# Attention and a routed expert layer on one core: q, k and v in natural token order, six batches of q and k turned by DMA, and a written order of issue

## The chip, the cores and the metric

The kernel runs on one core of one Trainium2 chip. A core has four compute engines that each run their own stream of instructions in order: TensorE (PE in the profile, with its weight loads as PEld), VectorE (DVE), ScalarE (ACT) and GpSimd (POOL). SyncE (SP) issues most of the DMAs here, in order too, and sixteen DMA engines move the data. The metric is the device time of one execution in microseconds, as a median of several runs.

## The reference, cut to what matters

```python
# q, k, v: (8 batches, 8 heads, 576 tokens, 64), f: (8, 8, 576), all float32
scores = q @ k.T / 8                                # per batch and head
cum = np.cumsum(np.log(np.clip(f, 1e-4, 1.0)), -1)
scores = where(causal, -1e9, scores + cum[:, None] - cum[None, :])
attn = softmax(scores)                              # over keys
x[b] = concat over heads of attn @ v                # (576, 512) per batch
logits = x @ w_gate                                 # 8 experts
for each token, in order:                           # sticky routing
    e = argmax(logits) if first token or sigmoid(x @ w_local) < 0.5 else e of the token before
    out = softmax(logits)[e] * (relu(x @ w1[e]) @ w2[e])   # 512 -> 1024 -> 512
```

All products are made of float16 parts: each operand is split into a high part and a low part (the rest), and the products of the parts that count are added up in PSUM.

## The kernel before, in words

**Stages.** Attention runs over eight batches, one after the other, and the batches overlap at their edges. Then the experts run, first two with fixed places, then the other six in the order of their loads. While attention runs, the routing of finished batches is worked out in between.

**Attention of a batch.** Per batch there are 21 units: 20 of 512 score columns and a small one (`d2unit`). A unit goes through stages on different engines: `sc` (TensorE makes scores into a PSUM bank, from the tiles `A` and `B` of q and k, `scores`, line 931), `mx` (VectorE takes the negative maximum, `negmax`, 948), `ex` (ScalarE takes exp, `expo`, 967), `tr` (TensorE transposes P, 984), `hi` (ScalarE casts to float16, 989), `lo` (VectorE makes the rest, 993; in three to five units a batch TensorE subtracts, `sub`, 996, and ScalarE casts, `lo2`, 1001), `av` (TensorE multiplies with v, 963), and for the last unit of a pair `n1` and `n2` (VectorE divides by the sum, 1024 and 1028). PSUM has four banks for scores, two for `tr`, two for the output of `av`.

**Order of tokens.** The 512 main tokens of a batch are loaded two neighbours to a partition (`load_main`, 190: runs of 512 bytes; v in `load_v`, 205: runs of 256 bytes), so keys and queries of one chunk are interleaved. The code undoes that in the access patterns of `queries` and `keys` (919, 924), with `ORD3` and `ORD4` (18), and in a store of P with a step of two (`expo`). The routing works on the tokens in that order and turns them back with small products (`rows`, 1462, `back`, 1508).

**Preparing q and k.** For the batch after the running one, GpSimd splits q and k into parts (`hi_lo`, 352, lines 357 and 361) in a tile `t16`. For batches 1 to 7, TensorE transposes the 36 blocks of each into score banks (`tq`, 505) and ScalarE or VectorE evicts them into `A` (`eq`, 514, 516, 518; the factor of q is applied here); after that a DMA copies the high half of `A` into `B` (`copy_hi`, 419 to 425, `copy_last`, 429). Batch 0 is turned partly by `turn` (406), a DMA transpose of SBUF into SBUF. The output of a batch, x, goes the same way: split by GpSimd, turned by DMA transposes (`xt`, 814; `xlt`, 851), stored to DRAM (820).

**What sets the order.** While the program is built, `issue` (1301) keeps a model of the engines' clocks with estimated costs and picks, step by step, the stage that could start first, with weights and ranks of its own for each batch (`TUNE`, 79). GpSimd's work is doled out by `pump` (364), loads by `ship` (346) and transfers by `hold_back`. What follows attention (the end of the routing, the first expert tiles, weights) is ordered in the same way by `flow` (2148). On the chip, each engine then runs its stream as issued and waits on semaphores.

Of the kernel before, what the change touches and what calls it, by code (L numbers as in the profile page):

```python
# [17 lines left out]
ORD3, ORD4 = (0, 2, 1), (0, 2, 1, 3)  # L18
# [18 lines left out]
SUBS = (7, 11, 14, 16)  # L37


def moves_of(d):  # L40
# [3 lines left out]

# [4 lines left out]
GM, GW = 8, 500  # L49

SW = (-700, 0, 0)
LI = (14, 18)
PX = 6
XI = 3

TS = {"q": (13, 17, 18, 19, 20), "k": (19, 20, 20, 21, 21)}
TE = {"q": "ADDDA", "k": "DAAAD"}

UO = tuple(range(25))
# [36 lines left out]
}  # L96

# [5 lines left out]
def kernel(  # L103
# [13 lines left out]
    B, H, S, D = q.shape  # L117
# [64 lines left out]
    mask(mB, 0.0, 2, [[-1, 2], [-2, 64]], 1, ALU.not_equal, BIG)  # L182
    mask(mA, 0.0, 2, [[1, 2], [2, 64]], -1, ALU.is_ge, -BIG)


# [4 lines left out]
    def load_main(b, nm, C, h0, h1, eng=nc.sync):  # L190
        src = (q, k)["qk".index(nm)]
        eng.dma_start(
            out=LT[b, nm][:, 4 * h0:4 * h1, :].rearrange("p (h C r) d -> p C h (r d)", C=2, r=2)[:, C],
            in_=src[b, h0:h1, C * 256:(C + 1) * 256].rearrange("h (p r) d -> p h (r d)", r=2))

    def load_last(b, nm, eng=nc.sync):
        src = (q, k)["qk".index(nm)]
        for r in range(2):
            eng.dma_start(out=LT[b, nm][r * 64:(r + 1) * 64, 32:36, :],
                              in_=src[b].rearrange("(j r) s d -> r s j d", r=2)[r, 512:576])  # L200
# [4 lines left out]
    def load_v(b, eng=nc.sync, groups=((0, H),), last=True, cs=range(4)):  # L205

        if (b, "v") not in LT:
            new_load(b, "v")
        t = LT[b, "v"]
        for h0, h1 in groups:  # L210
            for c in cs:
                eng.dma_start(out=t[:, 8 * c + h0:8 * c + h1, :],
                              in_=v[b, h0:h1, c * 128:(c + 1) * 128].rearrange("h s d -> s h d"))
        for u in range(2 if last else 0):
            eng.dma_start(out=t[u * 64:(u + 1) * 64, 32:36, :],
                          in_=v[b].rearrange("(m u) s d -> u s m d", u=2)[u, 512:576])
# [14 lines left out]
    for h0, h1 in ((0, 2), (2, 4)):  # L231
        for nm in "qk":
            for C in range(2):
                load_main(0, nm, C, h0, h1)


    for c in range(2):
        nc.gpsimd.memset(QB[0][64:70, 16 * c + 8:16 * c + 16], -1.0)
# [85 lines left out]
    def nop():  # L324
        pass


    queue = deque()
    quota = [0.0]

    bulk = deque()

    held = []

    def hold_back(ready, fn):
        held.append((ready, len(held), fn))

    def let_go(t):
        while held:
            x = min(held)  # L340
            if x[0] > t:
                return
            held.remove(x)
            x[2]()

    def ship(i):
        while bulk and bulk[0][0] <= i and bulk[0][1]():
            bulk.popleft()[2]()
            if i < 99:
                break  # L350

    def hi_lo(hi, lo, t, n):

        m, w = t.shape[1], 1
        for d in t.shape[2:]:
            w *= d
        out = [(m * w, lambda: nc.gpsimd.tensor_scalar(hi, t, 1.0, 1.0, ALU.mult, ALU.mult))]
        for i in range(0, m, n):
            e = min(i + n, m)
            out.append((2 * (e - i) * w,  # L360
                        lambda i=i, e=e: nc.gpsimd.tensor_tensor(lo[:, i:e], t[:, i:e], hi[:, i:e], ALU.subtract)))
        return out

    def pump(left):

        quota[0] += sum(c for c, _ in queue) / max(left, 1)
        while queue and (queue[0][0] <= quota[0] or left <= 0):
            c, fn = queue.popleft()
            quota[0] -= c
            clock["POOL"] = max(clock["POOL"], clock["PE"]) + 1.1 * c  # L370
            fn()
# [11 lines left out]
    def aug_main(b, nm, h0, eng=nc.sync):  # L383
        B, src = Tq[b][nm + "B"], augm[:, b * H + h0:(b + 1) * H]
        if nm == "k":
            eng.dma_start(out=flat(B[64:67, 4 * h0:32]), in_=src.rearrange("j h x -> j (h x)"))
        for c in range(2 if nm == "q" else 0):
            eng.dma_start(out=flat(B[67:70, 16 * c + 2 * h0:16 * c + 16]).rearrange("p (g x) -> p g x", x=64),
                          in_=src.rearrange("j h (a c x) -> j c (h a) x", a=4, c=2)[:, c])
# [16 lines left out]
    def turn(b, nm, h0, h1):  # L406
        t16, A = Tq[b][nm + "t"], Tq[b][nm + "A"]
        if nm == "k":
            nc.sync.dma_start_transpose(out=A[:, 4 * h0:4 * h1], in_=flat(t16[:, 4 * h0:4 * h1]))
            return  # L410
        for c in range(2):
            nc.sync.dma_start_transpose(
                out=A[:, 16 * c + 2 * h0:16 * c + 2 * h1, :].rearrange("p a (r x) -> p (a r) x", r=2),
                in_=flat(t16[64 * c:64 * c + 64, 4 * h0:4 * h1]))
# [4 lines left out]
    def copy_hi(b, nm, h0, h1):  # L419
        A, B = Tq[b][nm + "A"], Tq[b][nm + "B"]  # L420
        if nm == "k":
            nc.sync.dma_start(out=B[0:64, 4 * h0:4 * h1], in_=A[64:128, 4 * h0:4 * h1])
            return
        dst, src = (t[0:64, 0:32].rearrange("p (c h C) x -> p c h (C x)", c=2, C=2)[:, :, h0:h1] for t in (B, A))
        nc.sync.dma_start(out=dst, in_=src)
# [9 lines left out]
    def prep_qk(b, nm):  # L435

        def begin():
            new_prep(b, nm)
            prep_aug(b, nm)
            if nm == "q":  # L440
                scale_q(b, 0, 16)
                clock["ACT"] += 950

        def turns(h0):
            if nm == "q" and h0 == 0:
                scale_q(b, 16, 36)
                clock["ACT"] += 1150
            if nm == "k" and h0:
                turn(b, nm, h0, h0 + 5)
            else:  # L450
                turn(b, nm, h0, h0 + 4)
                if h0:
                    turn_last(b, nm)

        def half(g0, g1):
            R = {}

            def parts(i):
# [212 lines left out]
    def moves(x):  # L671
# [1957 lines left out]
```

## Time and profile before

| | us |
|---|---|
| median of 3 runs | 798.42 |
| lowest and highest | 796.38, 800.25 |
| the profiled execution | 794.33 |
| its span, first to last instruction | 792.6 |

The page of the profile gives each engine's busy time and share of the span, the share in 40 slices, the DMA queues, the chain that ended last and the costliest groups of instructions. A busy time is the union of the instructions' own spans. For TensorE a span goes from a matmul's start to its modelled end, and matmuls overlap, so a busy TensorE isn't one at its peak. "DMA share" is the mean busy share of the sixteen DMA engines; packets of one engine overlap, so it can go above 1. The chain that ended last holds only the last 22 us (stores of the last outputs), so the readings below go by stretches.

### The profile page before, as it was taken

The numbers are of one execution on the slowest core, as the hardware profiler recorded it, in microseconds if no ns is written. First come the engines' busy times: TensorE is split into PE (matmuls) and PEld (weight loads), VectorE is DVE, ScalarE is ACT, GpSimd is POOL, SyncE is SP. The second block draws the span as 40 slices with busy tenths as digits, with TensorE's granted clock in tenths as the row PEclk, the third lists the DMA queues.
The fourth block names the chain that finished last, engine by engine and source line by source line (L and its number), as shares of the span: only waits on it lengthen the run. The fifth ranks groups of instructions, "written<-read, shape, count | busy, mean of one in ns | idle before, by whom it ended". The sixth has DMA issues, their size and how long they took to land. (4 is left out here: it accounts for less than half of the span.)

```text
span 792.6 us, 22037 instructions
## 1 busy us (share of the span) xinstructions
PE 744.1 (94%) x8972; PEld 540.2 (68%) x8972; DVE 496.6 (63%) x1097; ACT 435.6 (55%) x813; POOL 409.5 (52%) x525
## 2 busy tenths in 40 slices
PE   5799979998998989988899999999999999999996
PEld 2687868787887868877684576675665757666453
DVE  6789869899988989799769734252450514325010
ACT  5798969797886968875634125242341524324121
POOL 9799989395986779759608414222302213030101
PEclk9999999999999999998999999999999999999998
DMA  7968998877959677295594395574482854727101
GB/s 180 190 144 196 202 188 183 169 142 168 168 139 165 154 154 135 49 197 154 108 223 184 84 266 138 162 213 160 137 206 78 200 168 163 204 89 201 42 2 51
DMA packets 195338, 122.01 MB, mean 154 GB/s; under 512 B 135099, under 2 KB 171197, under 8 KB 195212
## 3 DMA queue, kind: packets, MB, share of 16 engines
q1 hardware_dynamic: 189169, 101.42, 57.0%
q0 software_dynamic: 6064, 19.14, 7.1%
q8 instruction: 72, 1.18, 0.6%
q14 instruction: 33, 0.27, 0.1%
HBM read 72.15 MB, written 19.36 MB: 115 GB/s over the span
## 5 line engine op out<-in xcount | busy, mean ns | idle before, releaser
L969 ACT ACTIVATE P<-st,nm 128x512 f32<-128x512 f32 (+3 forms) x288 | 153.3, 587 | 25.4 <-DVE nm L949 20.2
L1766 PE MATMUL z<-xT,wh 128*128 128x300 f16 (+7 forms) x832 | 144.6, 289 | 0.3 <-DVE hl L1753 0.3
L949 DVE TENSOR_REDUCE nm<-st 128x1 f32<-128x512 f32 (+4 forms) x264 | 133.8, 543 | 12.7 <-PE st L945 5.5
L989 ACT CAST ph<-pt 128x512 f16<-128x512 f32 (+1 forms) x200 | 115.8, 584 | 39.4 <-PE pt L984 33.8
L984 PE MATMUL pt<-ident,P 128*128 128x128 f32 x784 | 123.9, 281 | 9.1 <-DVE pl L993 5.7
L993 DVE TENSOR_TENSOR pl<-pt,ph 128x512 f16<-128x512 f32 (+1 forms) x171 | 114.0, 671 | 15.1 <-ACT ph L989 11.5
L1758 POOL DMA_INDIRECT out_dram<-o,ranki x23 | 23.9, 1039 | 160.9 <-ACT o L1757 139.8
L1753 DVE SCALAR_TENSOR_TENSOR hl<-z,hh 128x240 f16<-128x240 f32 (+7 forms) x64 | 42.3, 662 | 96.3 <-ACT hh L1752 94.7
L984 PEld LDWEIGHTS pt<-ident,P 128*128 128x128 f32 x784 | 85.3, 143 | 24.6 <-DVE pl L993 6.6
L1793 PE MATMUL y<-uh,hh 128*128 128x512 f16 (+2 forms) x440 | 101.1, 310 | 0.3 <-ACT o L1757 0.2
L1793 PE MATMUL y<-ul,hh 128*128 128x512 f16 (+2 forms) x440 | 100.8, 309 | 0.0
L1793 PE MATMUL y<-uh,hl 128*128 128x512 f16 (+2 forms) x440 | 100.8, 309 | 0.0
L1766 PEld LDWEIGHTS <-wh 128*128 128x128 f16 x832 | 80.9, 97 | 26.6 <-issue 0.9
L1766 PE MATMUL z<-xT,wl 128*128 128x300 f16 (+7 forms) x416 | 94.4, 289 | 0.0
L1793 PEld LDWEIGHTS <-hh 128*128 128x128 f16 (+2 forms) x880 | 57.0, 100 | 53.4 <-issue 5.4
L963 PE MATMUL xp<-VH,pl 128*128 128x65 f16 (+1 forms) x960 | 90.5, 195 | 2.5 <-DVE pl L993 1.8
L963 PE MATMUL xp<-VH,ph 128*128 128x65 f16 (+1 forms) x960 | 91.7, 196 | 0.0
L963 PE MATMUL xp<-VL,ph 128*128 128x65 f16 (+1 forms) x960 | 91.2, 195 | 0.0
L963 PEld LDWEIGHTS <-ph 128*128 128x128 f16 (+1 forms) x1920 | 84.6, 102 | 7.6 <-issue 4.0
L1752 ACT ACTIVATE hh<-z 128x240 f16<-128x240 f32 (+7 forms) x64 | 36.7, 574 | 91.7 <-PE z L1766 87.4
L938 PE MATMUL st<-KB,QB 70*128 70x256 f16 (+4 forms) x448 | 77.2, 280 | 4.3 <-DMA KB<-Ak 4.3
L938 PE MATMUL st<-Ak,Aq 128*128 128x256 f16 (+4 forms) x448 | 77.0, 282 | 2.9 <-ACT P L969 2.5
(371 smaller groups left out, 1407.4 us busy)
## 6 DMA issues: line engine op xcount, KB each, us to landing
stg<-in_moe_w_dram SPq DMA_DIRECT2D x64, 512.0 KB
xs<-xr SPq DMA_DIRECT2D x16, 512.0 KB
ldq<-in_q_dram SPq DMA_DIRECT2D x14, 512.0 KB
ldk<-in_k_dram SPq DMA_DIRECT2D x14, 512.0 KB
ldv<-in_v_dram SPq DMA_DIRECT2D x28, 256.0 KB
QB<-Aq SPq DMA_DIRECT2D x15, 256.0 KB
KB<-Ak SPq DMA_DIRECT2D x15, 256.0 KB
ldv<-in_v_dram SPq DMA_DIRECT2D x20, 64.0 KB
```

The source lines that it names most:

```text
L938: nc.tensor.matmul(st[p0:p0 + m, co:co + n], lhsT=queries(lq, kk, h, c), rhs=rhs, start=(ps == 0 and first and co == col), stop=(ps == 1), ...
L949: nc.vector.tensor_reduce(dst, src, axis=AX.X, op=ALU.max, negate=True)
L963: nc.tensor.matmul(xo, lhsT=a[:, c0:c0 + m], rhs=w[:, vi, :], start=False, stop=(i == n - 1 and jj == 2), skip_group_check=True)
L969: nc.scalar.activation(P[:, c0:c1].rearrange("p (k x r) -> p k r x", r=2, x=64), st[:, c0:c1].rearrange("p (k r x) -> p k r x", r=2, x=64) ...
L984: nc.tensor.matmul(U["pt"][:, i * 128:(i + 1) * 128], lhsT=P[:, i * 128:(i + 1) * 128], rhs=ident, is_transpose=True, start=(i == 0), stop ...
L989: nc.scalar.copy(U["ph"][:, :cols], U["pt"][:, :cols])
L993: nc.vector.tensor_tensor(U["pl"][:, :cols], U["pt"][:, :cols], U["ph"][:, :cols], ALU.subtract)
L1752: nc.scalar.activation(hv, z[:, 0:nh, 0:wd], AF.Relu)
L1753: nc.vector.scalar_tensor_tensor(lv, z[:, 0:nh, 0:wd], 0.0, hv, ALU.max, ALU.subtract)
L1758: nc.gpsimd.indirect_dma_start(out=outf, out_offset=bass.IndirectOffsetOnAxis(ap=scat(t), axis=0), in_=o, in_offset=None, bounds_check=NT ...
L1766: nc.tensor.matmul(z[:, a, 0:wd], lhsT=w[:, d, fc * 128:(fc + 1) * 128], rhs=xT[:, x, a * wd:(a + 1) * wd], start=(i == 0), stop=(i == len ...
L1793: nc.tensor.matmul(y[m * r:m * r + m, 0:w], lhsT=a[:, fc, c0:c0 + m], rhs=u[:, fc, w * r:w * r + w], start=(i == 0), stop=(i == len(prods) ...
```

## The change

- **Layout.** The host hands q, k and v over as (batch, 128 partitions, 36 groups, 64), tokens in natural order (`laid`), so a load reads one contiguous run per partition. `queries`, `keys`, `ORD3`, `ORD4`, `expo`, the masks, the copies of q, the decay rows and the routing's products follow; a batch's v is loaded by three DMAs and q and k by three each.
- **Turning.** For batches 2 to 7, `prep_turned` issues two DMA transposes each for q and k (`turn`, 16 and 20 blocks) in place of `tq` and `eq`; ScalarE scales q before the split (`scale_q`, two instructions a batch). Batch 1 is still turned by TensorE (`by_tensor`).
- **Order.** The scheduler, its costs and weights are gone. `ORDER` has one letter for each step of attention, `THEN` one for each step of what follows; `issue` and the last loop read them off. Each step still waits on semaphores on the chip.
- **Routing.** `rows` has two products in place of four, `back` and the carries one each on full 128-row tiles, and the reordering copy `so` is gone.

```diff
-ORD3, ORD4 = (0, 2, 1), (0, 2, 1, 3)
+ORD3, ORD4 = (0, 1, 2), (0, 1, 2, 3)
...
+PARTS = dict(zip("SMNETHLUKARW tc 0123hz gr d. qkfuy xjils vbpe".replace(" ", ""), (
+    "sc mx mn ex tr hi lo sub lo2 av n1 n2 tq eq z0 z1 z2 z3 zh zl gate side due next "
+    "Tq Tk qs cq ck X L x l s v b p e").split()))
+ORDER = (
+    "SSMSMddMEddSTEMSHSdLTEMAHdSLTEMAHSMETLESHMSELTAEMSHMTSEMALHdSRELTWSHMTEALHSUREWTKMSHMdTEMAAHLtTEtLAcMHAcLRTSTW"
...
+THEN = (
+    "gggbbgbhhhbbbggbbbbbihbbgbbbcjgghjbbgbhhhhhgghbgbhhbhbbibbgdhjhbjjjbhhhiibhbbhbigbggbbggkkbbbbgghgjbbbbgebggbb"
...
     def load_main(b, nm, C, h0, h1, eng=nc.sync):
         src = (q, k)["qk".index(nm)]
-        eng.dma_start(
-            out=LT[b, nm][:, 4 * h0:4 * h1, :].rearrange("p (h C r) d -> p C h (r d)", C=2, r=2)[:, C],
-            in_=src[b, h0:h1, C * 256:(C + 1) * 256].rearrange("h (p r) d -> p h (r d)", r=2))
+        g0, g1 = (4 * (h0 + (h1 - h0) * x // 2) for x in (C, C + 1))
+        eng.dma_start(out=LT[b, nm][:, g0:g1], in_=src[b, :, g0:g1])
...
+    def load_v3(b, c):
+        if c == 0:
+            new_load(b, "v")
+        g0, g1 = ((0, 16), (16, 32), (32, 36))[c]
+        nc.sync.dma_start(out=LT[b, "v"][:, g0:g1], in_=v[b, :, g0:g1])
...
     def turn(b, nm, h0, h1):
         t16, A = Tq[b][nm + "t"], Tq[b][nm + "A"]
-        if nm == "k":
-            nc.sync.dma_start_transpose(out=A[:, 4 * h0:4 * h1], in_=flat(t16[:, 4 * h0:4 * h1]))
-            return
...
+        nc.sync.dma_start_transpose(out=A[:, 4 * h0:4 * h1], in_=flat(t16[:, 4 * h0:4 * h1]))
...
+    def prep_turned(b, nm):
+
+        def begin():
+            new_prep(b, nm)
+            prep_aug(b, nm)
+
+        if nm == "q":
+            part["qs"].extend(lambda g=g: scale_q(b, *g) for g in ((0, 16), (16, 36)))
+        part["T" + nm].extend(lambda h=h: turn(b, nm, *h) for h in ((0, 4), (4, 9)))
+        part["c" + nm].extend([lambda: copy_hi(b, nm, 0, 4), lambda: copy_hi(b, nm, 4, 8), lambda: copy_last(b, nm)])
+        return [begin] + halves(b, nm, 0, 16) + halves(b, nm, 16, 36)
...
-            return t[:kk, 16 * (c % 2) + 2 * h + c // 2]
+            return t[:kk, 4 * h + c]
...
         def expo(P, st, c0, c1, bias):
 
-            nc.scalar.activation(P[:, c0:c1].rearrange("p (k x r) -> p k r x", r=2, x=64),
-                                 st[:, c0:c1].rearrange("p (k r x) -> p k r x", r=2, x=64), AF.Exp, bias=bias)
+            nc.scalar.activation(P[:, c0:c1], st[:, c0:c1], AF.Exp, bias=bias)
...
+    def issue(last=False):
+
+        for x in order:
+            st = PARTS[x]
+            if st in runs:
+                go_on(st)
+            elif st != "next":
+                part[st].popleft()()
+            if st in ("sc", "next") and not last:
+                return
...
         def back():
             R["ps"] = bank()
-            for j, x in enumerate((R["so"].rearrange("p r x -> p (r x)"), R["sc"])):
-                nc.tensor.matmul(R["ps"][:, 0:GC], lhsT=x, rhs=idc[:, j], start=(j == 0), stop=(j == 1),
-                                 skip_group_check=True)
+            nc.tensor.matmul(R["ps"][:, 0:GC], lhsT=scw[:, 0:128], rhs=ident16[:, 0:GC], start=True, stop=True,
+                             skip_group_check=True)
...
+def laid(name, a):
...
+    if name not in ("q", "k", "v"):
+        return a
...
+    main = a[:, :, :512].reshape(b, h, 4, 128, d).transpose((0, 3, 2, 1, 4) if name == "v" else (0, 3, 1, 2, 4))
+    last = a[:, :, 512:].reshape(b, h // 2, 2, 64, d).transpose(0, 2, 3, 1, 4)
+    return _np.concatenate([main.reshape(b, 128, 32, d), last.reshape(b, 128, 4, d)], axis=2)
```

The counts that the prediction uses from the diff: the letters of `ORDER` hold 12 `Tq` and 12 `Tk` (two each for six batches), 12 `qs`, 10 `tq` and 10 `eq` (batch 1 only), and as many attention stages as before (192 `sc`, 200 `tr`, 171 `lo`, 29 `sub`).

## Rows read from the trace of the kernel before

**Rows 1.** The page's first part: busy time, share of the span, instructions.
```profile
PE 744.1 (94%) x8972; PEld 540.2 (68%) x8972; DVE 496.6 (63%) x1097; ACT 435.6 (55%) x813; POOL 409.5 (52%) x525
```

**Rows 2.** By stretch, busy us: PE, PEld, DVE, ACT, POOL; granted clock, DMA share, GB/s.
```profile
28.00:396.30 368.30, 341.08 (x5773) 286.07 (x5774) 321.39 (x768) 291.55 (x596) 284.56 (x344) 0.98 0.77 159
75.50:305.00 229.50, 215.38 (x3701) 182.28 (x3700) 203.01 (x485) 186.77 (x383) 176.29 (x228) 0.99 0.83 167
396.30:793.00 396.70, 386.73 (x3063) 243.72 (x3060) 154.72 (x296) 126.49 (x186) 99.11 (x132) 0.99 0.53 148
160.30:209.50 49.20, 46.52 (x773) 38.77 (x772) 47.51 (x114) 41.39 (x86) 36.55 (x47) 1.00 0.76 157
209.50:245.80 36.30, 35.36 (x686) 30.80 (x684) 32.95 (x81) 29.71 (x61) 28.92 (x33) 1.00 0.72 153
```

**Rows 3.** Waits of PE, DVE and ACT, 20 to 410 us: total, times, longest.
```profile
PE pt L984 <- DVE pl L993: 5.7, 12, 1.1
PE st L938 <- DMA KB<-Ak: 4.3, 2, 3.0
DVE pl L993 <- ACT ph L989: 11.5, 21, 1.5
ACT ph L989 <- PE pt L984: 33.8, 52, 3.2
```

**Rows 4.** Turning q and k, groups by line: count, busy us, mean ns, idle before.
```profile
L505 PE MATMUL st<-ident,t16q 128*128 128x128 f16 x252 | 19.4, 219 | 0.2
L514 ACT ACTIVATE Ak<-st 128x1024 f16<-128x1024 f16 x21 | 21.4, 1034 | 1.1 <-PE st L505 1.1
L514 ACT ACTIVATE Aq<-st 128x1024 f16<-128x1024 f16 (+1 forms) x14 | 11.6, 826 | 0.9 <-PE st L505 0.9
L516 DVE TENSOR_SCALAR Aq<-st 128x1024 f16<-128x1024 f16 x21 | 14.1, 682 | 0.8 <-PE st L505 0.8
L518 DVE COPY Ak<-st 128x1024 f16<-128x1024 f16 (+1 forms) x14 | 7.6, 546 | 0.0
```

**Rows 5.** Timeline of PE, 16 transposes in a row: start, length.
```profile
234.94 1.06 PE L505 MATMUL st<-ident,t16q 128*128 128x128 f16 x16
```

**Rows 6.** ScalarE from SBUF float32, 1024 columns, among the groups by line.
```profile
L1965 ACT ACTIVATE wh<-stg 128x1024 f16<-128x1024 f32 x26 | 27.1, 1048 | 0.4 <-DMA stg<-in_moe_w_dram 0.4
```

**Rows 7.** The transposes of x: SP's issue (ns min/median/max), and a stretch with two.
```profile
L814 SPq DMA_TRANSPOSE xt<-xr x16: 1752/2852/3666, 80.9 to 397.1; - x16
339.59 6.02 SPq L814 DMA_TRANSPOSE xt<-xr  x2
339.60:346.00 6.40, 6.29 (x116) 4.75 (x117) 5.80 (x19) 3.44 (x9) 2.56 (x4) 1.00 1.07 158
```

**Rows 8.** Stretches with a load of q, of k, and of weights.
```profile
259.90:267.00 7.10, 6.84 (x101) 5.72 (x99) 6.91 (x18) 6.50 (x15) 6.93 (x7) 1.00 0.68 175
267.40:275.40 8.00, 7.70 (x149) 6.99 (x147) 6.26 (x21) 6.92 (x16) 3.61 (x5) 1.00 0.59 150
362.00:368.00 6.00, 4.72 (x79) 3.77 (x80) 5.68 (x13) 4.23 (x12) 5.71 (x6) 0.69 0.94 307
```

**Rows 9.** By stretch: TensorE idles, its clock falls; first and last of three.
```profile
248.00:252.00 4.00, 2.19 (x17) 1.27 (x15) 4.00 (x10) 2.93 (x8) 2.83 (x3) 0.96 1.38 220
252.00:256.00 4.00, 4.00 (x30) 3.60 (x31) 3.44 (x8) 2.02 (x4) 3.17 (x4) 0.61 1.36 142
364.00:370.00 6.00, 5.43 (x71) 4.40 (x68) 4.21 (x10) 4.70 (x11) 5.67 (x6) 0.53 0.70 242
```

**Rows 10.** Batch 0's start: a stretch in which TensorE waits for a copy.
```profile
32.00:35.50 3.50, 0.90 (x12) 0.86 (x13) 0.86 (x2) 0.36 (x1) 0.16 (x1) 1.00 1.12 223
```

**Rows 11.** Groups by line and shape: the routing's copy, exp, a contiguous store.
```profile
L1506 DVE COPY so<-sc 10x128 f16<-10x128 f16 x4 | 2.1, 534 | 0.0
L969 ACT ACTIVATE P<-st,nm 128x512 f32<-128x512 f32 x96 | 71.0, 745 | 18.4 <-DVE nm L949 13.7 <-DVE G L1458 1.5 <-ACT ph L989 0.8
L1757 ACT ACTIVATE o<-y,rank 128x512 f32<-128x512 f32 x23 | 15.7, 685 | 81.0 <-PE y L1793 72.1 <-PEq L2576 4.8 <-issue 4.0
```

More of the change, by code (lines that the diff above doesn't have):

```diff
@@ L211, in load_v @@
             for c in cs:
[L212 to L216, printed above, removed]
+                eng.dma_start(out=t[:, 8 * c + h0:8 * c + h1], in_=v[b, :, 8 * c + h0:8 * c + h1])
+        if last:
+            eng.dma_start(out=t[:, 32:36], in_=v[b, :, 32:36])
+    def load_v3(b, c):
[3 more added lines that the diff above has]
+        nc.sync.dma_start(out=LT[b, "v"][:, g0:g1], in_=v[b, :, g0:g1])
     pers = (per0, per1)
@@ L528, in ready @@
-        def ready(js):
-            return (0, lambda: turns.extend(group(j) for j in js))
-        return [(0, begin)] + half(0, 16) + [ready((0, 1))] + half(16, 36) + [ready((2, 3, 4))]
+            part["tq"].append(tq)
+            part["eq"].append(eq)
+        for j in js:
+            group(j)
+            if j in (1, 3):
+                part["c" + nm].append(lambda j=j: copy_hi(b, nm, 2 * j - 2, 2 * j + 2))
+            elif j == 4:
+                part["c" + nm].append(lambda: copy_last(b, nm))
@@ L561, in prep, with loads @@
-        return q + [mark("q")] + k + [mark("k")] + v + last
+        part["p"].extend(prep_turned(b, "q") + prep_turned(b, "k") + prep_v(b))
+        part["v"].extend(lambda c=c: load_v3(b, c) for c in range(3))
+        if b == 2:
+            part["p"].append(init_route)
+        if b + 1 < B:
+            loads(b + 1, "q")
+            loads(b + 1, "k")
+    def loads(b, nm):
+        part["b"].extend([lambda: (new_load(b, nm), load_main(b, nm, 0, 0, H)), lambda: load_main(b, nm, 1, 0, H),
+                          lambda: load_last(b, nm)])
@@ L695, in moves @@
         elif a == "2":
-            c = lambda: all((1, x, j) in turned for x in 'qk' for j in range(4))
-            def some(C):
-                if C == 0:
-                    new_load(2, b)
-                if C < 2:
-                    load_main(2, b, C, 0, H)
-                else:
-                    load_last(2, b)
-            bulk.extend([(0, c, lambda C=C: some(C)) for C in range(3)])
+            loads(2, b)
         elif a == "R":
@@ L1159, in then @@
         def then(i, f, *args):
-            eng, cost, last, takes, frees = units[i]["n2"]
+            last = units[i]["n2"]
             def both():
@@ L1164, in both @@
                 f(*args)
-            units[i]["n2"] = eng, cost, both, takes, frees
+            units[i]["n2"] = both
         for j in range(4):
@@ L1253 @@
-    SHUTS = "add", "rows2", "hold", "scan1", "onehot", "place2", "invert2", "pinvert2", "fill2"
-    chain = deque()
-    side = {"end": (0.0, "PE"), "run": None, "cost": None}
+            then(18, some)
+            then(19, lambda: F[2]())
+        return units
+    pools = {}
+    runs = {"gate": None, "side": None}
     def whole(fn):
@@ L1331, with go_on @@
[L1331 to L1356 removed]
+    def go_on(st):
+        if runs[st] is None:
+            runs[st] = iter(part[st][0]() or ())
+        if next(runs[st], whole) is whole:
+            part[st].popleft()
+            runs[st] = None
@@ L1359 @@
+    order = iter(ORDER)
+    def issue(last=False):
[6 more added lines that the diff above has]
+            if st in ("sc", "next") and not last:
+                return
+    def step(u):
+        for st, fn in u.items():
+            part[st].append(fn)
+        issue()
     GC = NCH // 4
@@ L1719, in early_weights @@
             if n == 0:
-                out += [(0, lambda i=i: load(i)) for i in blocks[0:2]]
+                out += [lambda i=i: load(i) for i in blocks[0:2]]
             if n + 2 < len(blocks):
-                out.append((0, lambda i=blocks[n + 2]: load(i)))
+                out.append(lambda i=blocks[n + 2]: load(i))
             out += pieces(i)
@@ L1801, in experts, with run @@
             f()
-    def run(steps, todo=(), at=None, share=1200):
+    def run(steps, todo=(), at=None):
         todo = list(todo)
@@ L1926 @@
+            if b > 0 and i == 0:
+                part["gate"].extend(gate(b - 1))
                 if b % 2 == 0:
                     steps, EX["rest"] = route(b // 2 - 1, False)
-                    chain.extend(steps)
+                    part["side"].extend(steps)
                 if b == B - 4:
-                    chain.append(first_idx)
+                    part["side"].append(first_idx)
                 if b == B - 2:
-                    chain.extend([early_idx, early_tok])
-    issue()
@@ L1934 @@
-    let_go(1e12)
-    pump(0)
-    ship(99)
-    while chain:
-        side_issue(*side_next())
+                    part["side"].extend([early_idx, early_tok])
+    issue(True)
     pctx.close()
@@ L2242, in fn @@
                 e = n > 1
-                if e and part == 0 and n == 2:
+                if e and which == 0 and n == 2:
                     HID["hh", 1] = ep.tile([128, NF, M1], F16, name="hh")
@@ L2354, in routing, with t2 @@
[L2354 to L2367 removed]
+        def t2():
+            nc.vector.tensor_copy(flat(xlt), R["ps"])
@@ L2394 @@
-    pump(0)
+    streams = dict(zip("bcdefghijklmnop", (
+        products(), hidden(0), hidden(1), outputs(0), outputs(1), routing(), third_pair(), blocks(FW), second(), second_rest(),
+        fetch(CAP4[0] - 4 * EARLY, lambda i: EX["ga"][:, EARLY + i:EARLY + i + 1], "x0"),
+        fetch(CAP4[1] - 4 * EARLY, lambda i: EX["ga"][:, e0 + i:e0 + i + 1], "x1l"), ranking(), third(), steps_of([constants]))))
+    for x in THEN:
+        next(streams[x])
     sidx, xp_, wpb = EX["sa"], EX["xp"], EX["wpb"]
```

831 lines of the change are left out of this document (193 added, 638 removed), and 16 rows, old and new, of the table TUNE.

## The prediction

> **What bounds the kernel now.** I read the page's engine totals first [rows 1]. TensorE looks busy for 94% of the span, but its spans overlap: sixteen transposes in a row take 1.06 us, though each is listed with 219 ns [rows 4, 5]. So one costs (1.06 - 0.22) / 15 = 56 ns of the engine, and the rest is a tail that the busy time counts at every stall. The totals also average over stages, so I went to the stretches [rows 2]. Behind 396.3 us, in the experts, TensorE is busy for 386.7 of 396.7 us and VectorE for 39%: that part is TensorE's own, and the change doesn't touch its products. The change lives in 28 to 396.3 us: eight batches of 46.0 us each. There TensorE is busy for 92.6% (tails included), VectorE for 87.3%, ScalarE 79%, GpSimd 77%. In the batch at 160 us VectorE reaches 96.6%, in the next 90.8%. The waits say that no engine is alone: TensorE waits for VectorE's `pl`, VectorE for ScalarE's `ph`, ScalarE for TensorE's `pt`, each in many short waits [rows 3]. So attention is a ring of TensorE, VectorE and ScalarE, in which VectorE has the most real work, and its length is VectorE's work divided by the share that the order of issue lets it reach. The DMA engines are the fifth party: mean share 0.83 in 75.5 to 305 us [rows 2], and the two waits of scores for a copy into `KB` are theirs [rows 3].
>
> **The change part by part.** First, what leaves. The 504 transposes and 70 evictions belong to seven batches, and six go [rows 4] (k's 252 transposes are a like group). TensorE: 432 x 56 ns = 24.2 us. VectorE: (14.1 + 7.6) x 6/7 = 18.6 us. ScalarE: (21.4 + 11.6) x 6/7 = 28.3 us. Four score banks no longer serve for turning, which can only help.
>
> The routing's copy `so` leaves VectorE 2.1 us, three quarters of it in attention: 1.6 us [rows 11]. The other routing products are a few short ones each; I count nothing.
>
> What comes instead. ScalarE scales q: 1024 and 1280 columns, by the nearest row [rows 6] 1.05 + 1.31 = 2.36 us a batch, 14.1 us for six, so ScalarE is still relieved by 14.2 us; its 21% of idle time covers it. This adds a wait: the scaling waits for q's load, behind it on ScalarE stand the `ex` and `hi` of the running units, and VectorE waits for those; GpSimd's split of q now waits for the scaling, with the splits of k, v and x behind it. Price: nothing if the load is some 10 us old, up to 3.0 us apiece, like the longest wait for a copy [rows 3], if it is late. In the letters the loads stand several units ahead of the scaling, so I take nothing and leave the rest to the range.
>
> The store of exp becomes contiguous. A contiguous ScalarE store of 512 columns takes 685 ns, the strided exp 745 [rows 11]: between nothing and 60 ns a unit, on an engine with idle time, so nothing. Natural order lets some pairs of score products become one with the same columns; the trace doesn't show that a product costs more than its columns, and I count nothing there too.
>
> DMA. A batch's transposes are 2 x 36 blocks. The nearest stretch turns 32 blocks of x in 6.4 us at a share of 1.07 [rows 7], 6.8 us of all sixteen engines, 0.21 us a block, so 15.4 us a batch; SP's shortest issue of 16 blocks, 1.75 us [rows 7], bounds it from below at 7.9. I take the stretch, as it is the same form. The loads shrink: a load of q or k (1.18 MB) takes 0.68 x 7.1 = 4.8 or 0.59 x 8.0 = 4.7 us of the engines [rows 8]; at the rate of the weights, whose rows are contiguous too (307 GB/s at 0.94), it is 3.6 us, so three loads give back 3.5 us (v is read in shorter runs and may give more). DMA time a batch: 0.83 x 45.9 = 38.1 [rows 2], plus 15.4, minus 3.5, is 50.0 us. That fits into 42 us only at a share of 1.19. Rows show 1.12 and 1.38 where much is queued [rows 9, 10]. SP issues four more transposes a batch, 2.85 us each by the median, in order with loads, copies into `B` and the transposes of x, and each of these stands behind a transpose that waits for GpSimd's split. I price the crowding at 1.5 us, between nothing and the 7.8 or more of the rivals below.
>
> [...]
>
> The written order. [...] From below, a share of 85%; from above, the 96.6% of one batch [rows 2]. I take 88%, close to the present mean of 87.3%, as the work on TensorE falls with VectorE's and a batch edge loses its late turning.
>
> The start. Scores wait 3.0 us for the copy into `KB` while the DMA share is 1.12 [rows 3, 10]; shorter loads in batch 0 take away between nothing and 3.0 us: 1.5 us.
>
> What follows attention: TensorE idles for 10 us there [rows 2], the last stores among it; I take nothing.
>
> **The sum.** VectorE's work in attention: 321.4 - 18.6 - 1.6 = 301.2 us. At 88% that is 342.3 us against 368.3: -26.0. Start -1.5, crowding +1.5. Total -26.0, from 794.3 to 768.3 us. From the other side, if TensorE sets the length, its 24.2 us give nearly the same. The profiled execution is 4.1 us below the median of 798.4, so the forecast for a median is 772 us. At 85% attention is 354.4 us (-14, median 784), at 90.8% 331.7 us (-37, 762).
>
> **The rivals.** (1) The order of issue lifts VectorE to 91 to 96.6%: 331.7 to 311.8 us, 742 to 762. For it: batches that reached that [rows 2]. Against it: the DMA time above. (2) The DMA engines become the bound at the share of 1.12 seen at the start [rows 10]: 50.0 / 1.12 = 44.6 us a batch in place of 45.9, so 6 x 1.3 = 7.8 us and the start's 1.5 are all that is won: 789. For it: the sum of DMA time; against it: the 1.38 and 1.36 of [rows 9], and that part of a share is packets that overlap. (3) It doesn't do what it says: the new steps are bound elsewhere or the gain is eaten at the batch edges, 795 to 802. (4) Slower: the DMA engines give no more than a share of 1.0 when transposes, copies and loads alternate. Then a batch takes 50.0 us, 6 x 4.1 - 1.5 = 23 us more: 821. It decides at 50.0 / 45.9 = 1.09: below that share the change loses. [...] For it: 0.83 already, transposes slower than loads by the byte [rows 7, 8]; against it: the shares over 1.1.
>
> [...]
>
> **How the numbers follow.** Forecast (share 85 to 91%) 0.48, rival 1 0.17, rival 2 0.20, rival 3 0.06, rival 4 0.09. Within 0.5% (4 us, about what a measurement of this kernel can tell from no change) is rival 3: 0.06; slower is rival 4: 0.09; faster is the rest, 0.85. The range of 8 in 10 runs from 752 (leaving the upper part of rival 1, some 0.07) to 792 (leaving rivals 3 and 4 for the most part).
>
> **What would show it.** In the profile after: no group for `st<-ident,t16` but batch 1's 72, VectorE's work in attention near 301 us, its share 85 to 91%; attention's last unit some 26 us earlier and the experts' stretch as long as before; DMA share in the middle batches near 1.1 with few waits of scores for `KB` or `QB`. Long waits there, or of ScalarE for `ldq`, mean rival 2 or 4; a share over 91% means rival 1. The prediction is wrong if the experts' stretch changes by more than some us, or if GpSimd, with 77%, turns out to be what the units wait for.

## The result, and the profile after

The changed kernel takes 770.11 us, the median of 4 runs (768.36 to 774.67), beside 797.4 us for the kernel before on the same chip (4 runs, 794.69 to 800.25): a ratio of 0.9666, 95% interval 0.9609 to 0.9723. The forecast was 772. The profiled execution took 768.85 us, its span 766.8.

The page's first part of the changed kernel, the counterpart of [rows 1]:

```profile
PE 716.1 (93%) x8400; PEld 507.9 (66%) x8400; DVE 478.0 (62%) x1055; ACT 416.1 (54%) x795; POOL 409.9 (53%) x515
```

By stretch, with the columns of [rows 2]; attention's last unit now ends at 369.15 us (before at 396.3), and the second line is five whole batches, as 75.5 to 305 us were:

```profile
28.00:369.15 341.15, 316.75 (x5281) 257.56 (x5281) 305.97 (x738) 274.48 (x584) 280.11 (x331) 0.98 0.96 213
70.65:277.53 206.88, 192.98 (x3234) 155.99 (x3232) 186.66 (x456) 171.04 (x366) 169.15 (x207) 0.98 1.01 217
369.15:767.00 397.85, 382.50 (x2987) 239.85 (x2986) 151.80 (x287) 124.24 (x180) 103.95 (x135) 0.98 0.53 147
```

Attention took 341.2 us in place of 368.3, and the experts' stretch 397.9 in place of 396.7. So the whole gain lies in attention. VectorE's work there fell from 321.4 to 306.0 us, TensorE's busy time from 341.1 to 316.8, and the DMA share rose from 0.77 to 0.96.

The groups of turning that are left, the scaling of q and the exp of 512 columns (count, busy us, mean ns, idle before):

```profile
L400 PE MATMUL st<-ident,t16q 128*128 128x128 f16 x36 | 2.7, 219 | 0.1
L378 ACT ACTIVATE ldq<-ldq 128x1024 f32<-128x1024 f32 (+1 forms) x12 | 14.1, 1171 | 1.2 <-DMA ldq<-in_q_dram 1.2
L816 ACT ACTIVATE P<-st,nm 128x512 f32<-128x512 f32 x95 | 65.9, 703 | 9.6 <-DVE nm L890 7.5 <-DVE nm L796 1.5 <-DVE rs L861 0.5
```

The 252 transposes of q are 36, the scaling costs the 14.1 us that were counted and waits 1.2 us in all, and exp takes 703 ns in place of 745.

The waits of 20 to 400 us, as [rows 3], show more waits for copies than before, but short ones:

```profile
PE pt L830 <- DVE pl L839: 3.2, 6, 1.4
PE st L785 <- DMA KB<-Ak: 6.9, 4, 2.1
PE st L785 <- DMA QB<-Aq: 2.7, 2, 1.7
DVE pl L839 <- ACT ph L835: 11.1, 23, 1.5
ACT ph L835 <- PE pt L830: 34.9, 61, 3.5
```

All of this fits the forecast: a share of VectorE of 306.0 / 341.2 = 89.7% where 88% was taken. It doesn't show that VectorE's work is why. The experiments were made for that.

### The profile page after: what moved, and what is told of

Its sections match the earlier page's. It is cut to its first block, busy times and chain, and to the rows that moved or that the text cites. A ratio compares the mean times of both kernels' runs of the same rounds, so it can differ in the third digit from the quotient of the medians.

```text
span 766.8 us, 20737 instructions
## 1 busy us (share of the span) xinstructions
PE 716.1 (93%) x8400; PEld 507.9 (66%) x8400; DVE 478.0 (62%) x1055; ACT 416.1 (54%) x795; POOL 409.9 (53%) x515
## 5 line engine op out<-in xcount | busy, mean ns | idle before, releaser
L816 ACT ACTIVATE P<-st,nm 128x512 f32<-128x512 f32 (+3 forms) x288 | 144.0, 561 | 14.5 <-DVE nm L890 7.5
L835 ACT CAST ph<-pt 128x512 f16<-128x512 f32 (+1 forms) x200 | 113.1, 587 | 36.9 <-PE pt L830 34.9
L830 PE MATMUL pt<-ident,P 128*128 128x128 f32 x784 | 117.7, 281 | 8.2 <-DVE pl L839 3.2
L839 DVE TENSOR_TENSOR pl<-pt,ph 128x512 f16<-128x512 f32 (+1 forms) x171 | 111.9, 667 | 11.9 <-ACT ph L835 11.1
L1434 POOL DMA_INDIRECT out_dram<-o,ranki x23 | 24.2, 1050 | 158.4 <-ACT o L1433 142.1
L1429 DVE SCALAR_TENSOR_TENSOR hl<-z,hh 128x240 f16<-128x240 f32 (+7 forms) x64 | 42.4, 662 | 96.2 <-ACT hh L1428 94.6
L810 PE MATMUL xp<-VH,pl 128*128 128x65 f16 (+1 forms) x960 | 88.8, 195 | 2.6 <-DVE pl L839 2.3
L810 PE MATMUL xp<-VH,ph 128*128 128x65 f16 (+1 forms) x960 | 89.7, 196 | 0.0
L810 PE MATMUL xp<-VL,ph 128*128 128x65 f16 (+1 forms) x960 | 89.3, 195 | 0.3 <-issue 0.3
L810 PEld LDWEIGHTS <-ph 128*128 128x128 f16 (+1 forms) x1920 | 82.6, 103 | 7.5 <-issue 4.0
L785 PE MATMUL st<-KB,QB 70*128 70x512 f16 (+5 forms) x384 | 77.2, 300 | 9.6 <-DMA KB<-Ak 6.9
L785 PE MATMUL st<-Ak,Aq 128*128 128x512 f16 (+5 forms) x384 | 77.1, 303 | 0.8 <-DVE nm L890 0.3
```

Source lines behind the costliest of these rows:

```text
L785: nc.tensor.matmul(st[p0:p0 + m, co:co + n], lhsT=queries(lq, kk, h, c), rhs=rhs, start=(ps == 0 and first and co == col), stop=(ps == 1), ...
L810: nc.tensor.matmul(xo, lhsT=a[:, c0:c0 + m], rhs=w[:, vi, :], start=False, stop=(i == n - 1 and jj == 2), skip_group_check=True)
L816: nc.scalar.activation(P[:, c0:c1], st[:, c0:c1], AF.Exp, bias=bias)
L830: nc.tensor.matmul(U["pt"][:, i * 128:(i + 1) * 128], lhsT=P[:, i * 128:(i + 1) * 128], rhs=ident, is_transpose=True, start=(i == 0), stop ...
L835: nc.scalar.copy(U["ph"][:, :cols], U["pt"][:, :cols])
L839: nc.vector.tensor_tensor(U["pl"][:, :cols], U["pt"][:, :cols], U["ph"][:, :cols], ALU.subtract)
```

## The experiments

Each ratio is to the kernel before, run on the same chip. "DMA time" is DMA share times length, from 28 us to the end of attention's last unit: 283.6 us in the kernel before, 0.96 x 341.2 = 327.5 in the changed one. As the share goes above 1 (1.38 in [rows 9]), it is a measure to compare runs by, not pure work.

### TensorE turns again, with three ways to evict

In the changed kernel, `prep_turned` puts the groups of `by_tensor` behind the same letters, and a small function inserts the letters of `tq` and `eq` into `ORDER` by rule (and leaves out those of `qs`):

```diff
-        if nm == "q":
-            part["qs"].extend(lambda g=g: scale_q(b, *g) for g in ((0, 16), (16, 36)))
-        part["T" + nm].extend(lambda h=h: turn(b, nm, *h) for h in ((0, 4), (4, 9)))
+        part["T" + nm].extend(lambda js=js: by_tensor(b, nm, js) for js in ((0, 1), (2, 3, 4)))
...
+ORDER = spread(ORDER)
```

> The changed kernel (natural layout, contiguous loads, written order), but q and k of batches 2 to 7 are turned by TensorE again, one group of blocks behind an exp, with the evictions shared between VectorE and ScalarE as in the kernel before; the scaling of q goes back into the eviction. Theory W (VectorE's work over its share sets attention's length): VectorE gets 18.6 us back, over a share of 0.90 that is +20.7, less some us for 15.4 us of DMA time a batch that goes: 785 to 791. Theory P (TensorE's work sets it): 432 x 56 ns = 24.2 us over TensorE's share: about 790 to 795, so this run doesn't part W and P, the next two do. Theory O (the written order and the layout bring the gain, the turning by DMA little): 770 to 775.

> As e1_tensor_turns, but in batches 2 to 7 all ten evictions of a batch go to ScalarE. VectorE's work is then that of the changed kernel, TensorE's that of e1, and ScalarE gets 6 x 9.5 - 14 = 43 us more than in the changed kernel, 317 us. Theory W: 770 to 776. Theory P: as e1, 785 to 795. Theory A (ScalarE's work over a like share of 0.9): 317 / 0.9 = 352 in place of 341 us: 781.

> As e1_tensor_turns, but in batches 2 to 7 all ten evictions of a batch go to VectorE: 8 x 0.68 + 2 x 0.42 = 6.3 us a batch, 37.7 us for six, over what the changed kernel has. Theory W: 37.7 / 0.9 = +42: about 810. Theory P: as e1, 785 to 795. Theory O: 770 to 780.

Measured: e1 800.02 us, ratio 1.0046 (1.0017 to 1.0076); e2 801.11, 1.0060 (1.0034 to 1.0086); e3 801.39, 1.0058 (1.0032 to 1.0083). Attention by stretch, e1, e2 and e3 (columns of [rows 2]):

```profile
28.00:397.70 369.70, 340.05 (x5713) 279.86 (x5713) 321.10 (x768) 288.47 (x602) 278.54 (x331) 1.00 0.63 158
28.00:400.20 372.20, 343.62 (x5713) 282.44 (x5713) 306.00 (x738) 310.96 (x632) 278.65 (x331) 0.99 0.63 157
28.00:401.70 373.70, 342.54 (x5713) 281.82 (x5713) 335.91 (x798) 263.71 (x572) 278.86 (x331) 0.99 0.62 156
```

VectorE's work is the third busy time, behind PE and PEld: 321.1, 306.0, 335.9 us. Thirty us of work on it make no difference to the time, and its share moves freely from 0.82 (e2) to 0.90 (e3). Theory W falls, as e2 has the changed kernel's work on VectorE and is 30 us slower. (ScalarE's work went the other way, 311.0 to 263.7 us, so what work on VectorE alone costs is left to e6.) What the three share is the turning on TensorE, whose busy time goes up by 23.3 us in e1, and the order that the function makes. Two more things follow. Layout and written order without turning by DMA, in that order, bring nothing (e1 against the kernel before). And with them in place, turning by DMA is worth about 30 us, though it adds 327.5 - 0.63 x 369.7 = 94.6 us of DMA time.

### Turning by DMA in the kernel before

The kernel before with `turn`, `scale_q` and `copy_hi` in place of `tq` and `eq` for batches 2 to 7 (e4); then the same with q, k and v laid out by the host so that each load reads one run per partition, in the old order of tokens (e11). The scheduler's model got 4.5 us from the split to the end of a transpose; q is turned in pieces of 64 rows there, as the old `turn` does.

```diff
+        def turns(h0):
+            t = clock["POOL"]
+            hold_back(t + 200, lambda: turn(b, nm, h0, h0 + 4))
...
+            hold_back(t + 4500, lambda: copy_hi(b, nm, h0, h0 + 4))
...
+                turned[b, nm, j] = t + 4500
```

> The kernel before, its layout and its scheduler kept, but q and k of batches 2 to 7 are turned by DMA (and q scaled by ScalarE), placed by the scheduler's model. Theory W: VectorE's 321.4 - 18.6 = 302.8 us over the mean share of before, 0.88: 344 in place of 368, so about 774 to 778. Theory O (order and layout bring the gain): no better than 790 to 800. Theory D (the DMA engines take it back as long as the loads are in short runs): 38.1 + 15.4 = 53.5 us a batch over 1.12 = 47.8 in place of 45.9, 805 to 812.

> As e4_before_dma (the kernel before with its scheduler, q and k of batches 2 to 7 turned by DMA), but q, k and v are loaded in one long run per partition, in the kernel before's own order of tokens. Theory D: some 7 us of DMA time a batch go from e4's 865: 805 to 820, still over the kernel before, as q's transposes stay in pieces of 64 rows. Theory O (what e4 lacks is the written order): 850 to 865. Theory L (the loads were all that stood against turning by DMA): 770 to 785.

Measured: e4 865.49 us, ratio 1.0857 (1.0791 to 1.0922); e11 833.45, 1.0501 (1.0435 to 1.0568). The waits of TensorE for copies into `KB` in e4 (20 to 460 us) and in e11 (20 to 430 us), and attention of e4 and of e11 by stretch:

```profile
PE st L973 <- DMA KB<-Ak: 28.5, 5, 10.0
PE st L969 <- DMA KB<-Ak: 19.7, 4, 8.8
28.00:452.80 424.80, 338.39 (x5297) 273.78 (x5298) 313.93 (x737) 278.50 (x576) 281.82 (x342) 0.90 0.88 170
28.00:420.60 392.60, 329.41 (x5296) 267.92 (x5297) 311.25 (x736) 277.42 (x576) 281.50 (x342) 0.94 0.88 183
```

The same work taken off VectorE and TensorE made this kernel 69 us slower: attention grew by 56.5 us (424.8 - 368.3), and what follows it by 14.7, of which 7.5 us are a wait of TensorE for the last `xlt`. Long runs give back some 30 us (28.3 us of DMA time: 0.88 x 424.8 - 0.88 x 392.6). In what remains the DMA share is 0.88, below the 0.96 of the changed kernel, so the engines' capacity alone doesn't explain it. But in the five middle batches of e11 the share is 1.00:

```profile
67.97:310.26 242.29, 206.70 (x3340) 167.57 (x3340) 193.36 (x459) 178.37 (x371) 168.54 (x220) 0.94 1.00 200
```

That is 242.3 us of DMA time beside 1.01 x 206.9 = 209.0 in the changed kernel's, so the engines may have a part in it. The longest wait of e11, 8.84 us up to 116.4 us, shows another part. SP's issues before it, start and length (other lines left out), and the product of TensorE that waited:

```profile
100.69 3.52 SPq L405 DMA_TRANSPOSE Ak<-t16k  x1
...
107.67 4.29 SPq L405 DMA_TRANSPOSE Ak<-t16k  x1
112.01 1.27 SPq L413 DMA_TRANSPOSE Ak<-t16k  x1
113.33 1.24 SPq L418 DMA_DIRECT2D KB<-Ak  x2
...
116.40 0.59 PE L969 MATMUL st<-KB,QB 70*128 70x512 f16 x1 [8.84 <-DMA KB<-Ak]
```

The first four heads of k were turned from 100.69 us on, but their copy (one of the two at 113.33) stands in SP's queue behind the transposes of the other heads, and the next batch's first scores wait. So the order in which SP issues transposes and copies costs time: TensorE waits 19.7 us for `KB` in e11 and 6.9 in the changed kernel. How much of e11's some 63 us (833.45 - 770.11) over the changed kernel is this order, my 4.5 us, the pieces of 64 rows and the DMA time, these runs don't part.

### More work for one engine at a time

In the changed kernel, something that can be done twice without harm is done twice: the first transpose of P in each `tr` (e5), the product `n2` of the main tokens (e6), the exp of 128 columns in the units a (e7). The three edits, in that order:

```diff
+                nc.tensor.matmul(U["pt"][:, 0:128], lhsT=P[:, 0:128], rhs=ident, is_transpose=True, start=True, stop=True, ...)
...
+                for _ in range(1 if shape == [128, 4] else 2):
+                    nc.vector.tensor_tensor(to, N["xv"][..., 0:64], rb, ALU.mult)
...
+                for _ in range(2):
+                    expo(P, st, 0, 128, nm[:, h:h + 1])
```

> The changed kernel with work added to TensorE alone: the first block of P is transposed twice in each of the 200 tr stages, 200 x 117 ns = 23.4 us (four such transposes in a row took 0.63 us, one 0.28 us). Theory P (TensorE's work sets attention's length, as e1 to e3 suggest, where moving 30 us of evictions between VectorE and ScalarE changed nothing): about +24 us, 790 to 797. Theory B (in e1 to e3 it was the score banks held by the turning, not TensorE's work): +0 to +8 us. Theory W: 770 to 774. Theory R (a ring without a bound, in which work added anywhere passes about half): +12.

> The changed kernel with work added to VectorE alone: the 64 products n2 of the main tokens are made twice, 64 x 0.41 = 26 us. Theory W: 26 / 0.9 = +29 us. Theory P: +0 to +5. Theory R: +12.

> The changed kernel with work added to ScalarE alone: the exp of 128 columns in the 64 units a is made twice, 64 x 0.38 = 24 us. Theory W and theory P: +0 to +5. Theory R: +12.

Measured: e5 770.36 us, ratio 0.9642 (0.9579 to 0.9705); e6 777.8, 0.9735 (0.968 to 0.979); e7 773.09, 0.9665 (0.959 to 0.974). Attention of e5, e6 and e7:

```profile
28.00:371.60 343.60, 331.08 (x5482) 275.34 (x5478) 306.69 (x739) 277.40 (x584) 280.41 (x331) 1.00 0.96 212
28.00:374.10 346.10, 317.67 (x5281) 254.86 (x5281) 328.78 (x802) 275.35 (x584) 280.31 (x331) 1.00 0.94 209
28.00:373.30 345.30, 319.10 (x5281) 256.71 (x5281) 306.94 (x738) 293.88 (x646) 280.19 (x331) 1.00 0.96 210
```

Attention grew by 2.5, 5.0 and 4.2 us for 23, 26 and 24 us of work by count (the engine's busy time grew by 14.3, 22.8 and 19.4): 0.1 to 0.2 us for each. Among the ratios only e6's differs, by 0.7%, and its interval still touches the changed kernel's. No engine alone is the bound. W fails again, and P in its plain form too: e5 put TensorE at 331.1 of 343.6 us and cost next to nothing. The clock may hide some of the cost: its granted mean was 0.98 in the changed kernel's attention and 1.00 in all three, and what it lost there is 5.0 us (last section). Even with that added, it is 0.3 to 0.4 us for each us of work by count.

### More and less DMA time

e8 issues q's transposes of batches 2 to 7 twice. e9 gives the loads short runs again, by the host's layout and the patterns that read it. e10 leaves out q's transposes. e10's scores come from other batches' q, so its routing and its experts' stretch differ, and only its attention is read. The edits, in that order (e9's other loads likewise):

```diff
+        for _ in range(2 if b > 1 and nm == "q" else 1):
+            nc.sync.dma_start_transpose(out=A[:, 4 * h0:4 * h1], in_=flat(t16[:, 4 * h0:4 * h1]))
...
+        eng.dma_start(out=LT[b, nm][:, g0:g1].rearrange("p (g r) d -> p g (r d)", r=2),
+                      in_=src[b, g0 // 2:g1 // 2].rearrange("g p r d -> p g (r d)"))
...
+        part["T" + nm].extend(lambda h=h: nm == "k" and turn(b, nm, *h) for h in ((0, 4), (4, 9)))
```

> The changed kernel with DMA work added: the transposes of q of batches 2 to 7 are issued twice (36 blocks a batch more; from the DMA share of e1 and of the changed kernel, 0.63 x 369.7 = 233 and 0.96 x 341.2 = 328 us, two times 36 blocks take 15.8 us a batch). A batch then holds 43.3 + 7.9 = 51.2 us of DMA time. Theory D (DMA engines at a share of 1.12 are the bound): 51.2 / 1.12 = 45.7 in place of 42.6 us, +18 us. If they go to 1.2 or more under load: 0 to +6.

> The changed kernel, with q, k and v laid in DRAM so that the same DMAs read runs of 512 bytes (q, k) and 256 bytes (v), as in the kernel before, in place of one long run per partition. Nothing else differs: the same instructions on every engine and as many DMAs on SP. From the DMA share times length of e1 (233 us) and of the kernel before (284 us), short runs cost 51 us of DMA time in attention, some 7 us a batch. Theory D (the DMA engines are the bound of the changed kernel, at a share near 1.0): about +35 to +45 us, 805 to 815. Theory Q (in e8 it was SP's queue, in which the second transposes stood ahead of the copies into QB, not the DMA engines): 770 to 778. Theory W: 770 to 774.

> The changed kernel without the transposes of q in batches 2 to 7 (their scores use the tiles of q of batches 0 and 1; the split of q, its scaling and the copies into QB stay). 7.9 us of DMA time a batch and two transposes on SP go; no engine's work changes. Theory D: the DMA engines no longer set the length; the next bound, the ring of TensorE (share 0.93), VectorE (0.90) and ScalarE, gives 38 to 41 us a batch in place of 42.6: 745 to 762. Theory W: VectorE's work is the same, 766 to 772.

Measured: e8 823.91 us, ratio 1.0304 (1.0247 to 1.0362); e9 781.36, 0.983 (0.9769 to 0.989); e10's whole time is 842.99 (see above). Attention of e8, e9 and e10:

```profile
28.00:427.60 399.60, 333.35 (x5281) 268.37 (x5281) 304.19 (x738) 274.14 (x584) 279.39 (x331) 0.92 0.93 199
28.00:384.70 356.70, 320.02 (x5281) 260.88 (x5281) 304.60 (x738) 274.61 (x584) 280.03 (x331) 0.97 1.00 203
28.00:359.70 331.70, 313.86 (x5281) 255.13 (x5281) 304.32 (x738) 273.87 (x584) 280.32 (x331) 0.99 0.88 197
```

e9 is the clean test of the DMA engines, as every queue holds the same instructions: 356.7 - 327.5 = 29.2 us of DMA time more cost 15.5 us. (The expectation had 51 us; that was too much, see below.) By the medians it is 11.3 us. So in e9 the engines aren't a wall at share 1.0 but a drag: 0.4 to 0.5 us for each us of DMA time. e10 has 0.88 x 331.7 = 291.9, 35.6 us less, and gains 9.5 us, 0.3 for each; as it also takes twelve transposes out of SP's queue, that isn't the engines' share alone. e8 adds 0.93 x 399.6 - 327.5 = 44.1 us and loses 58.5, more than its DMA time, at a lower share than the changed kernel's. The waits of e8, of SP and of TensorE, 20 to 430 us:

```profile
SPq L363 <- DMA Aq<-t16q: 26.9, 12, 3.5
PE st L786 <- DMA KB<-Ak: 29.3, 7, 9.4
PE st L786 <- DMA QB<-Aq: 10.1, 6, 2.5
```

Each second transpose waits on SP for the first to land, as both write the same tile, and then has to be issued (3.0 us by the median of q's transposes in the changed kernel), with the copies into `QB` and `KB` behind it. By e9's price 44.1 us of DMA time are some 20 of the 58.5 us (an estimate); the larger part fits theory Q. But the wait of 26.9 us is the experiment's own, so e8 shows what a blocked SP queue costs, not what the queue costs the changed kernel.

### The frame of TensorE's turning without its work

> The changed kernel (q and k turned by DMA), to which the frame of e1's turning is added without its work: at the places where e1 turns a group of blocks, 60 times in batches 2 to 7, a score bank is taken, TensorE makes one 128x128 transpose of a constant in it (56 ns in place of 8 x 56), and VectorE or ScalarE copies those 128 columns out where e1 evicts 1024. 60 x 56 ns = 3.4 us of TensorE, some 60 x 0.2 us on the two others. Theory B (TensorE's turning costs the time since it holds a score bank and puts a step with two waits into the streams): most of e1's +30, so 785 to 800. Theory V (it is the amount of work on TensorE and in the evictions together, though each alone, in e5 to e7, cost 0 to 7 us): 770 to 776.

```diff
+            def tq(U=U):
+                U["pt"] = psS.tile([128, 8, 128], F16, name="st")
+                nc.tensor.transpose(U["pt"][:, 0], ident16, ident16)
...
+                    nc.scalar.copy(junk[0], U["pt"][:, 0])
...
+                    nc.vector.tensor_copy(junk[1], U["pt"][:, 0])
```

Measured: 774.28 us, ratio 0.9729 (0.9696 to 0.9762); attention in its profiled execution, the longest of the four, took 352.2 us, 11 more than the changed kernel's:

```profile
28.00:380.20 352.20, 323.66 (x5341) 262.63 (x5341) 307.72 (x767) 279.10 (x614) 279.02 (x331) 0.99 0.95 205
```

By the ratios the frame (a score bank, two waits, three short instructions, 60 times) explains about 5 of the 30 us, so theory B isn't the main part.

## Why the prediction was right, and where it wasn't

**The number** was right: 770.1 for 772, attention 341.2 for 342.3 us, the last unit 27.2 us earlier for 26, the experts within 1.2 us, scores waiting for `KB` 1.6 us at the start where it was 3.0 (forecast: 1.5 less). By the time, the forecast's case held, and rivals 1 to 4 didn't come.

**The step that carried it was wrong.** "VectorE's work divided by the share" treats the share as a property of the order. e2 and e3 show that work on VectorE can go from 306 to 336 us at nearly the same length; the share simply follows. e6 prices a us of VectorE's work at some 0.2 us of time, up to 0.4 if the clock hid 5.0 us there, so the relief of 20.2 us would be worth about 4 to 9 us by itself (an estimate from e6), not 26. I had written that TensorE's 24.2 us give nearly the same; that side is nearer to e1 to e3, where the turning on TensorE costs 30 us whoever evicts. The two sums agreed in size, and so a wrong cause gave a right number: that was luck. What the runs show in its place is the whole package: no gain without the turning by DMA (e1), a loss with it in the old layout and order (e4, e11), and 30 us between e1 and the changed kernel, of which no single engine's work explains more than a part.

**VectorE's work** was to be near 301 us and is 306.0. Early expert steps that the written order moves into attention are 2.4 us of that (seven `hl` in place of one); two operations of the routing are 4.3 more (below). The copies `so` gave back 1.1 us and not 1.6: the three in attention were shorter than the mean that was used.

**Transposes by DMA**, forecast 15.4 us a batch with a lower bound of 7.9: the kernel with them less e1 gives 94.6 / 6 = 15.8, e8 gives 2 x 44.1 / 6 = 14.7, e10 2 x 35.6 / 6 = 11.9. The stretch of [rows 7] was a good price, at the upper end. By the byte, 2.36 MB in 11.9 to 15.8 us are 149 to 198 GB/s, where that stretch, all its traffic counted, moved 158.

**What the layout gives back** was mis-sized: 3.5 us a batch in the forecast. The loads alone give 29.2 / 7 = 4.2 (e9) or 28.3 / 7 = 4.0 (e11). But from the kernel before to e1 it is (283.6 - 232.9) / 7 = 7.2, and in five middle batches, by e1's line below, 0.83 x 229.5 / 5 - 0.59 x 229.2 / 5 = 11.1. Where the rest comes from is open: of the 70,100 packets that e1 has fewer than the kernel before, e9 puts back 63,000, so some 7,000 lie outside the runs of the loads (the decay rows of q may be among them), and no run measured their time. So the DMA time of a middle batch was 1.01 x 206.9 / 5 = 41.8 us and not 50.0, and the decision point of 1.09 in rival 4 was put too high (41.8 / 45.9 = 0.91).

```profile
69.97:299.16 229.19, 210.72 (x3594) 174.09 (x3592) 198.85 (x481) 182.75 (x381) 168.76 (x208) 1.00 0.59 154
```

**The crowding** was priced at 1.5 us. Without half of the transposes (e10) attention is 9.5 us shorter, so it was mis-sized as well, by 8 us or more, hidden in a sum whose main term was too large for the wrong reason. What was to show rival 4, long waits of scores for `KB`, was real. It came with the old layout and another order in SP's queue: 28.5 us of such waits, in a kernel that lost 69 us (e4).

**The written order** was priced by VectorE's share, 85 to 91% (it is 89.7). Without DMA turning it brought nothing, with e1's inserted letters; its worth with DMA turning is part of the 63 us between e11 and the changed kernel. The stretches with a low clock lost 5.0 us of TensorE (last section), beside 6.1 in three stretches of the kernel before: 1.6 at 252 to 256 and 2.8 at 364 to 370 us [rows 9], 1.7 at 284 to 292 us (granted clock 0.73, then 0.85).

**The small terms held:** exp 42 ns shorter (0 to 60 was allowed), the scaling's wait 1.2 us in all, ScalarE's cover real (24 us more work on it cost 4.2 us, e7).

**The price of one block** speaks against the change: 56 ns of TensorE [rows 4, 5] against 0.17 to 0.22 us of DMA time (11.9 to 15.8 us for 72 blocks). The times of e4 and e11 went with that sign, the changed kernel's against it. Among what differs between e11 and the changed kernel are the order in SP's queue (TensorE waits 19.7 us for `KB`, and 6.9) and the DMA time (242.3 us in five batches, and 209.0).

**What stays open:** TensorE's turning costs about 30 us in e1, but its parts, added one by one, cost 0 (e5), 5 (e12) and a share of e6's and e7's 0 to 8, while e1 even frees 95 us of DMA time. Waits for copies aren't it either: TensorE waits 4.6 us for `KB` in e1, less than in the changed kernel. One reading is that the limit changes from batch to batch. In the batch from 70.65 to 105.06 us TensorE is busy for 34.12 of 34.41 us. There e5's 25 x 0.117 = 2.9 us lengthen it by 2.5, and e1's 4.0 us of transposes by 8.7, of which 2.6 is a wait for `KB`. In other batches e5's work fills stalls. That is argued from three profiles, not shown. And e1's letters were inserted by rule, not tuned, so part of the 30 us may be a poor order; no run tests that. The batch in the changed kernel and in e1:

```profile
70.65:105.06 34.41, 34.12 (x585) 28.17 (x583) 31.22 (x75) 32.75 (x70) 27.74 (x47) 1.00 0.98 203
69.97:113.04 43.07, 39.00 (x653) 32.39 (x651) 34.69 (x79) 35.00 (x72) 27.73 (x47) 1.00 0.45 125
```

## What to carry to other kernels

Find the bound by adding work that does no harm to one engine at a time, and compare the clock of the stretch as well; a high busy share, even 90%, didn't mean that the engine's work sets the time. Before moving work to DMA, lengthen the runs of the loads and look at what stands in the issuing queue behind each transpose: the same move cost 8.6% with short loads and late copies (e4) and, with both mended and the order written anew, belongs to a change worth 3.3%. When two sums from different causes agree, the agreement is no evidence for either; test the one by which you would decide next.

## What was unexpected in the hardware

**A short VectorE operation that took more than five times as long beside GpSimd.** `G`, 10 columns of float16 from two SBUF operands, took 164 and 161 ns for its two operations in the kernel before, with 20 columns, and 938 and 849 ns now (means of three in attention):

```profile
L1458 DVE TENSOR_TENSOR G<-is__182,kp 128x20 f16<-128x20 f16 x3 | 0.5, 164 | 0.0
L1460 DVE TENSOR_TENSOR G<-G,F 128x20 f16<-128x20 f16 x3 | 0.5, 161 | 0.0
...
L1146 DVE TENSOR_TENSOR G<-ones,kp 128x10 f16<-128x10 f16 x3 | 2.8, 938 | 0.0
L1148 DVE TENSOR_TENSOR G<-G,F 128x10 f16<-128x10 f16 x3 | 2.5, 849 | 0.0
```

The timeline of the changed kernel (start, length; other lines left out) shows what they run beside:

```profile
129.46 2.75 POOL L327 TENSOR_TENSOR t16k<-ldk,t16k 128x640 f16<-128x640 f32 x2
...
129.71 1.18 DVE L1146 TENSOR_TENSOR G<-ones,kp 128x10 f16<-128x10 f16 x1
130.92 1.32 DVE L1148 TENSOR_TENSOR G<-G,F 128x10 f16<-128x10 f16 x1
...
132.29 0.23 PE L1153 MATMUL st<-ident,G 128*128 128x128 f16 x1 [1.73 <-DVE G L1148]
```

The second `G` ends at 132.24 us, with GpSimd's split at 132.21; the first ends at 130.89, about the middle of GpSimd's two. The other four of attention end in the same way: two with such a pair (219.36 and 219.34, 305.62 and 305.59 us), two about the middle of one (221.60 and 307.84 us). The last two, behind attention at 379.4 and 380.0 us with GpSimd idle, take 0.16 us each. In the kernel before, GpSimd was idle beside five of the six; beside the other, from 149.41 to 149.58 us, its operation ended at 149.56. My reading is that `G` waited for GpSimd, so that some 4.3 us of VectorE's busy time in attention here are waiting (an estimate: 2.8 + 2.5 - 0.5 - 0.5). The trace shows the lengths and the ends; what held `G` up isn't shown.

**The clock may have hidden some of what was added.** TensorE idled 1.73 us for that `G`, and then ran at a low clock (columns of [rows 9], the changed kernel):

```profile
132.00:136.00 4.00, 3.71 (x28) 2.00 (x30) 3.49 (x9) 2.58 (x6) 3.92 (x5) 0.67 0.78 214
136.00:140.00 4.00, 4.00 (x56) 3.37 (x53) 2.17 (x6) 1.46 (x4) 3.83 (x5) 0.50 1.04 197
```

A second fall, at 196 to 204 us (0.78 and 0.80), makes it 5.0 us of TensorE lost in attention. In e5, with 23 us of work more on TensorE, the clock didn't fall at all (1.00 from 28 to 371.6 us), which may hide a part of what that work cost. It isn't shown that the work kept the clock up: in e6, with no more work on TensorE, the mean is 1.00 too.
